# A fused attention and expert kernel: two weight transposes made one, two turns of k moved into the next stage, stores moved to the end of their own stage

## The chip, the cores and the metric

The kernel runs on one core of one Trainium2 chip. The metric is device time in microseconds (us) for one execution. Each core has five engines that run their own instruction queues: TensorE (PE, with weight loads, PEld, beside its matmuls), VectorE (DVE), ScalarE (ACT), GpSimd (POOL) and SyncE (SP). SP computes nothing here: it issues transfers. The transfers themselves are carried out by the core's 16 DMA engines. Queue q1 holds those that SP issues (transposes, stores), q0 those that POOL issues (loads from memory with a cast).

## What is computed

Sliding-window causal attention (window 64, 8 batches, 8 heads, 576 rows, head size 64), and then a feed-forward layer on its output, with `h * cos(h)` as its activation:

```python
scores = scale * np.matmul(q, k.transpose(0, 1, 3, 2))
mask = (rel >= 0) & (rel < window)            # rel = row - column
scores = np.where(mask, scores, -1e9)
attn = softmax(scores); attn_out = np.matmul(attn, v)
x = attn_out.transpose(0, 2, 1, 3).reshape(B * S, H * D)   # 4608 x 512
h = x @ w_in                                                # 512 x 2048
out = (h * np.cos(h)) @ w_out                               # 2048 x 512
```

## The kernel before

The 4608 rows of x are worked in nine tiles `mt` of 512 rows (`n_mt`), and a batch has nine blocks of 64 rows (`NU`). A tile is eight blocks, so tile `mt` holds the last blocks of batch `mt - 1` and the first ones of batch `mt`. Each tile from 1 on is a stage of `T = 32` units of a plan: 16 units for the first product with its sine and gate (`L487` to `L491`, `L716`, `L719`), and 16 for the second (`L730`; tiles 7 and 8, `FAST`, use a product of seven parts, `L577`). In the profile a stage lasts about 31 us. While stage `mt = b - 1` runs its products, the attention of batch `b` is worked beside it:

- `load_chunk` (`L177`) loads q and k of a batch by POOL, in five chunks of 128 rows. `load_v` (`L185`) does the same for v.
- `turn_q` and `turn_k` (`L259`, `L270`, by `turn`, `L236`) transpose the chunks with DMAs issued by SP, in three turns each (`TURNS`, `L41`): chunks 0 and 1, chunks 2 and 3, and the short chunk 4. The tile for a turned k, `kT`, has two buffers.
- `burst_scores` (`L307`) puts all scores of half a batch on TensorE in two bursts per stage, at 14.6 and 20.2 units. The first burst takes blocks 0 to 3, the second the others (for batch 3 block 4 comes first in it, elsewhere block 8 last). Block j reads k's blocks j - 1 and j, and a chunk has two blocks.
- The weights of a batch come in nine groups, "places" 0 to 8. For each, `g_max` (DVE), `g_exp` (ACT), `g_inv` (DVE), `g_norm` (POOL, `L383`) and `g_trans` (`L396`) follow at fixed lags, of which the last issues a transposing DMA from SP (`L406`) into a tile `wT`. Some groups go through TensorE instead (`direct`).
- `values` (`L415`) multiplies the transposed weights by v on TensorE at the end of a stage, and `put_x` casts the result into the next tile of x.
- `store` (`L497`) writes 256 rows of a finished tile from `out_sb`, which has three buffers, by SP.

What runs when is written out by hand. For tile 0 and batches 0 and 1 the order is the string `FIRST`, in which `Gm.n`, `Ge.n`, `Gi.n`, `Gn.n`, `Gc.n` are the steps of group n and `V.p` the values of head pair p. Batch 1's groups 13 (four units) and 14 (three units) are those of pair 2. From tile 1 on, `at(time, step)` puts a step in a plan, and `pump(time)` (`L594`), called between TensorE's matmuls, emits every step that is due, sorted by time. Each engine's queue is then worked strictly in that order. This holds for SP's queue too: a transfer that waits for its data holds up all that stand behind it.

At the end of a stage that starts at unit `base`, with batch `b` in work, SP's order before the change is: wT of places 0 to 3, q's three turns for batch `b + 1`, wT of places 4 and 5, k's three turns for batch `b + 1` (26.0, 26.2, 26.4), wT of places 6 and 7, then, over the border, wT of place 8 (31.23), and the two stores of the tile just finished (32.5 and 33.5). Batch 2 has times of its own.

The tiles `s` and `e` (scores and exponentials of a group, 2 KB a partition) have six buffers each.

Of the kernel before, what the change touches and what calls it, by code (L numbers as in the profile page):

```python
# [10 lines left out]
def _safe_warn(msg, *a, **kw):  # L11
# [4 lines left out]
BF16 = mybir.dt.bfloat16  # L16
# [7 lines left out]
NU = 9  # L24
NC, NP = 6, 96
GF = 4
# [6 lines left out]
T = 2 * Q  # L33
LAGS = (0.2, 1, 3, 3.2, 3.8)
# [32 lines left out]
)  # L67
# [3 lines left out]
def kernel(  # L71
# [23 lines left out]
    att = ctx.enter_context(tc.tile_pool(name="att", bufs=3))  # L95
# [17 lines left out]
    st = {}  # L113
# [127 lines left out]
    def blocks_of(x, b, p, lo, n):  # L241
        if b < 2:
            return by_pair(x)[:, p, 64 * lo:64 * lo + 64 * n].rearrange("d (a t) -> d a t", t=64)
        at_ = [PAIRS * 2 * (i // 2) + 2 * p + i % 2 for i in range(lo, lo + n)]
        return x.rearrange("d (a t) -> d a t", t=64)[:, at_[0]:at_[-1] + 1:at_[-1] - at_[0] or 1]
# [33 lines left out]
    groups = [[(0, p, j) for j in range(GF * g, GF * g + GF)] for p in range(PAIRS) for g in range(TU // GF)]  # L279
# [19 lines left out]
    last = n_listed + 4, n_listed + 5  # L299
    direct = set(range(n_first)) | {n_first + i for i in DIRECT} | set(last)  # L300

    def keys(b, p, j):
        lo, chunks = max(j - 1, 0), 2 if j else 1
        rhs = blocks_of(st["kA", b], b, p, lo, chunks)
        return rhs[:, ::-1, :] if j and j % 2 == 0 else rhs, chunks
# [76 lines left out]

    def g_norm(n, engine="p"):  # L383
        (e, _), rden = st.pop(("e", n)), st.pop(("r", n))
        w = att.tile([128, GF, 128], BF16, tag="w", name="w", bufs=8)
        u = len(groups[n])
        (nc.gpsimd if engine == "p" else nc.vector).tensor_tensor(out=w[:, 0:u], in0=e[:, 0:u], op=ALU.mult,  # L387
                                in1=rden[:, 0:u].unsqueeze(2).to_broadcast([128, u, 128]))
        st["w", n] = w

    def put_wT(n, wT):
        for i, (b, p, j, *h) in enumerate(groups[n]):
            for e in range(2):
                st["wT", (b, 2 * p + e, j, h[0]) if h else (b, p, j, e)] = wT[:, i, 64 * e:64 * e + 64]

    def g_trans(n):  # L396
        w, u = st.pop(("w", n)), len(groups[n])
        if n in direct:
            st["tw", n] = t_ps = ps_t.tile([128, GF, 128], BF16, tag="t", name="tw_ps")
            for i in range(GF if n == FILL[0] else 0):  # L400
                nc.tensor.transpose(t_ps[:, i], ident, ident)
            for i in range(u):
                nc.tensor.transpose(t_ps[:, i], w[:, i], ident)
            return
        wT = att.tile([128, GF, 128], BF16, tag="wT", name="wT", bufs=20)
        nc.sync.dma_start(out=wT[:, 0:u], in_=w[:, 0:u].rearrange("p u c -> p (u c)"), transpose=True)  # L406
        put_wT(n, wT)

    def g_put(n, engine=None):
        wT, u = att.tile([128, GF, 128], BF16, tag="wT", name="wT", bufs=20), len(groups[n])  # L410
# [82 lines left out]
    def skewed(mt, ks, n):  # L493
        for ff in range(SKEW):
            first(mt, ff, ks, n == 0, n == PAIRS - 1)
# [95 lines left out]
    def at(time, fn, *args):  # L591
        plan.append((time, len(plan), fn, args))
# [8 lines left out]
    for i, (b, jobs, banks) in enumerate(bursts):  # L601
        t = T * (b - 1)
        at(t + BURST[i % 2] + 0.9 * (i == 1), burst_scores, i)
        for n in range(jobs[0][0], jobs[-1][-1] + 1):
            place = (n - n_listed) % NU
            time = t + BURST[0] + PACE * place
            lags = LAGS[:2] + tuple(t + T - 0.79 - time + 0.01 * s for s in range(3)) if place == NU - 1 else LAGS
            if b == 2 and place > 3:
                lags = tuple(max(x, y - time) for x, y in zip(lags, {4: (53.2, 53.5, 0, 0, 0), 5: (0,) * 5, 6: (0, 0, 60.96, 60.97, 61.5), 7: (0, 0, 61.1, 61.2, 61.8), 8: (61, 61.3, 0, 0, 0)}[place]))
            for lag, fn in zip(lags, (g_max, g_exp, g_inv)):  # L610
                at(time + lag, fn, n)
            at(time + lags[3], g_norm, n, "d" if n == n_listed + 5 else "p")
            if n in last:
                at(T * b - 4.1 + (n == last[1]), g_trans, n)
                at(T * b - 4.05 + (n == last[1]), g_put, n)
            else:
                at(time + lags[4], g_trans, n)

    for b in range(2, B):
        t0 = T * (b - 1)  # L620
        for lo, hi in TURNS:
            at(t0 - (2.01 - 0.1 * lo if b == 2 else T - (24.3 if b == 4 else 23.4) - 0.01 * lo), turn_q, b, lo, hi)
        if b > 2:
            for c in range(NB):
                for i, name in enumerate(("q", "k")):
                    time = 17.9 + 2.8 * i if b == 3 and c == NB - 1 else 5.6 + 1.6 * c + 0.8 * i
                    if name == "k" and (b == 3 or c > 2):
                        time = ((24.31 if c > 1 else 13) if b == 3 else 24.2 if b == 4 else 22.4) + 0.01 * c
                    if b > 4 and c == 0:
                        time = (24.26 if b == 5 else 22.46) + 0.01 * i - T  # L630
                    at(t0 - T + time, load_chunk, name, b, c)
        for lo, hi in TURNS:
            at(t0 + 0.1 * lo - (2 if b == 2 else 6), turn_k, b, lo, hi)
        for c in range(5):
            at(t0 + (8 if b == B - 1 else 0.5) + c, load_v, b, c)
        for half_ in range(2):
            if b == 2:
                at(t0 + 24.1 + 0.01 * half_, spread_v, b, half_, "p", 0, 2)
                at(t0 + 24.2 + 0.1 * half_, spread_v, b, half_, "p", 2, 4)
            else:  # L640
                at(t0 + (24 if b == 3 else 22.2) + 0.1 * half_, spread_v, b, half_)
    for mt in range(2, n_mt):
        for p in range(PAIRS):
            time = T * mt - (8.01 if mt == n_mt - 1 else 1.01)
# [55 lines left out]
    for mt in range(1, n_mt):  # L700
        base = mt * T
        gT = []
        for ks in range(PAIRS):
            pump(max([base - 1] + [time for time, _, fn, args in plan if fn is put_x and args[:2] == (mt, ks)]))
            skewed(mt, ks, ks)
        for ff in range(n_ff):
            for ks in range(PAIRS):
                if ff >= SKEW:
                    first(mt, ff, ks, ks == 0, ks == PAIRS - 1)
            h_ps = st.pop(("h", ff))  # L710
            sin = moe.tile([128, MT], F32, tag="sin", name="sin", bufs=4)
            if ff % 2 == 0:
                gt = moe.tile([128, 2, MT], BF16, tag="gT", name="gT", bufs=n_ff // 2 + 2)
                gT.append(gt)
            e = ff % 2
            nc.scalar.activation(sin, h_ps, AF.Sin, bias=math.pi / 2.0)  # L716
            if ff == n_ff - 1 and mt < B - 1:
                exp_table()
            nc.vector.tensor_tensor(out=gt[:, e], in0=h_ps, in1=sin, op=ALU.mult)  # L719
            pump(base + ff)  # L720
        if mt in FAST:
            fast_second(mt, gT)
            continue
        for ms0 in range(0, MT // 128, 2):
            o_sb = moe.tile([128, 2, d_model], F32, tag="out", name="out_sb", bufs=OUTS)
            o_ps = [bank(which, "out_ps") for which in (("O1",) if mt == n_mt - 1 and ms0 else ("O1", "O0"))]
            for e in range(2):
                ms = ms0 + e
                for ff in range(n_ff):
                    nc.tensor.matmul(out=o_ps[e], lhsT=gT[ff // 2][:, ff % 2, ms * 128:ms * 128 + 128],  # L730
                                     rhs=w_out_sb[:, ff], start=ff == 0, stop=ff == n_ff - 1)
                    if ff % 4 == 3:
                        if ff == n_ff - 1:
                            copy("a" if e and (mt > 1 or ms0) else "d", o_sb[:, e], o_ps[e])
                            if mt == n_mt - 1:
                                store(o_sb, mt, ms0, e, 1)
                        pump(base + Q + 4 * ms0 + (e * n_ff + ff) // 4)
            if mt < n_mt - 1:
                at(base + T + 0.5 + ms0 / 2, store, o_sb, mt, ms0, 0, 2)


# [28 lines left out]
```

## Time and profile before

| | |
|---|---|
| Median of 3 runs | 299.97 us (299.54 to 304.29) |
| The profiled execution | 300.91 us, its span 299.1 us |
| TensorE busy | 290.5 us, 2767 matmuls |
| ACT, DVE, POOL busy | 232.1, 229.3, 205.1 us |
| SP's transposes: wT, qT, kT | 60, 18, 18 |
| SP's stores of 512 KB | 16 |
| Queue q0 (POOL's loads) | 18.06 MB |
| Queue q1 (SP's transfers) | 25.15 MB |

The profile is one execution with all times from the start of the span. A row of a view that looks at some instructions gives engine, operation and tile, how often, the least, median and greatest duration in ns, and the first and last start in us; "DMA to landing" below it gives the least, median and greatest time from the issue of those transfers to the moment when their data lies at the goal. In a timeline a row begins with start and length of a run of equal instructions, and in square brackets stands how long the engine sat idle before it and for whom. In rows of windows follow the busy times of PE, PEld, DVE, ACT and POOL, the granted clock, the share of the DMA engines (over 1 where two queues are served at once) and GB/s. Waits are given as the total, how often, and the longest.

### The profile page before, as it was taken

The page shows a single profiled execution, that of the slowest core. Times are in us where ns is not written, and L with a number is a line of the kernel's source. Part 1 is how long each engine was busy: PE and PEld are TensorE (multiplying, and loading weights), DVE is VectorE, ACT ScalarE, POOL GpSimd, SP SyncE. Part 2 cuts the span into 40 slices and gives each one's busy share as a digit, 9 for nine tenths or more (in the row PEclk, how much of TensorE's full clock was granted, in tenths as well). Part 3 has the DMA queues.
Part 4 walks back from the last instruction along what each step waited for, and adds up shares of the span by engine and source line. Part 5 has one row for each costly group of instructions (what it writes and reads, how often), then busy time and mean ns, then how long its engine had stood idle before and what let it go on. Part 6 is the DMA issues. An engine that isn't in the chain of part 4 may idle for free.

```text
span 299.1 us, 8146 instructions
## 1 busy us (share of the span) xinstructions
PE 290.5 (97%) x2767; PEld 158.6 (53%) x2767; DVE 229.3 (77%) x896; ACT 232.1 (78%) x781; POOL 205.1 (69%) x226
## 2 busy tenths in 40 slices
PE   8979999899999999999999999999999999999995
PEld 3658854544454444444454545444544454784485
DVE  4988887888887885788677866887588658986893
ACT  4998699687988799769987998699969997305700
POOL 9899558982799959994999499959997850000000
PEclk9999999999999999999999999999999999999999
DMA  7999999999999999999999999999999443003013
GB/s 145 176 203 192 193 191 146 131 144 159 221 172 114 160 198 176 136 172 235 160 156 153 233 137 171 143 232 155 158 143 161 72 88 143 0 2 141 3 35 105
DMA packets 168267, 43.79 MB, mean 146 GB/s; under 512 B 155617, under 2 KB 163873, under 8 KB 168225
## 3 DMA queue, kind: packets, MB, share of 16 engines
q0 software_dynamic: 100896, 18.06, 80.7%
q1 hardware_dynamic: 67184, 25.15, 47.6%
q8 instruction: 21, 0.34, 0.5%
q14 instruction: 22, 0.17, 0.2%
q10 hardware_dynamic: 144, 0.07, 0.1%
HBM read 36.70 MB, written 9.44 MB: 154 GB/s over the span
## 4 chain that ended last, share of the span: by engine, by line
PE 75%; DMA 11%; POOL 5%; DVE 3%; ACT 3%; issue 1%; POOLq 0%; DVEq 0%
PE h_ps L490 37%; PE out_ps L730 23%; PE out_ps L577 8%; DMA w_out<-in_moe_w_out_dram 7%; DMA wT<-w 3%; ACT e L370 2%; PE o_ps L422 2%; PE s_ps L321 2%; POOL w L387 2%; DMA q<-in_q_dram 2%; PE out_ps L473 1%; POOL v L188 1%; POOL w_in L204 1%; DVE s L358 1%; DVE v L126 1%
## 5 line engine op out<-in xcount | busy, mean ns | idle before, releaser
L490 PE MATMUL h_ps<-xT,w_in 128*128 128x512 bf16 x512 | 111.8, 379 | 0.2
L719 DVE TENSOR_TENSOR gT<-h_ps,sin 128x512 bf16<-128x512 f32 x128 | 84.8, 688 | 27.2 <-ACT sin L716 27.2
L716 ACT ACTIVATE sin<-h_ps 128x512 f32<-128x512 f32 x128 | 73.7, 599 | 33.2 <-PE h_ps L490 32.5
L370 ACT ACTIVATE e<-s,negm 128x128 f32<-128x128 f32 (+1 forms) x256 | 97.1, 382 | 2.2 <-DVE negm L358 1.2
L387 POOL TENSOR_TENSOR w<-e,rden 128x512 bf16<-128x512 f32 (+1 forms) x68 | 68.8, 1028 | 29.6 <-DVE rden L380 21.0
L730 PE MATMUL out_ps<-w_out,gT 128*128 128x512 bf16 x384 | 85.3, 379 | 0.0
L490 PEld LDWEIGHTS <-w_in 128*128 128x128 bf16 x512 | 50.1, 98 | 59.1
L730 PEld LDWEIGHTS <-gT 128*128 128x128 bf16 x384 | 36.5, 98 | 43.1
L358 DVE CUSTOM_DVE_ANT_0 s<-s_ps,mask 128x128 f32<-128x128 f32 (+1 forms) x256 | 56.0, 276 | 2.5 <-PE s_ps L343 2.0
L370 ACT ACTIVATION_READ_ACCUMULATOR e<-s,negm 128x1 f32 x256 | 48.1, 188 | 0.0
L188 POOL DMA_DIRECT2D v<-in_v_dram x40 | 34.1, 877 | 1.2 <-PE h_ps L490 0.8
L182 POOL DMA_DIRECT2D q<-in_q_dram x30 | 26.3, 892 | 3.9 <-issue 3.3
L380 DVE RECIPROCAL rden<-den 128x4 f32<-128x4 f32 (+1 forms) x73 | 12.1, 166 | 18.4 <-ACT e L370 18.2
L182 POOL DMA_DIRECT2D k<-in_k_dram x30 | 26.2, 885 | 0.0
L126 POOL COPY v<-v 64x1536 bf16<-64x1536 bf16 (+3 forms) x16 | 22.9, 1431 | 0.4
L358 DVE DVE_READ_ACCUMULATOR2_ANT negm<- 128x1 f32 x256 | 21.2, 83 | 0.0
L126 DVE CAST xT<-o_ps 128x512 bf16<-128x512 f32 x24 | 15.6, 679 | 6.4 <-PE o_ps L422 6.2
L473 PE MATMUL out_ps<-w_out,gT 128*128 128x512 bf16 x64 | 15.0, 379 | 0.3 <-DMA w_out<-in_moe_w_out_dram 0.2
L454 PE MATMUL h_ps<-xT,w_in 128*128 128x256 bf16 x128 | 14.8, 273 | 0.0
L126 ACT CAST xT<-o_ps 128x512 bf16<-128x512 f32 x12 | 7.0, 582 | 8.5 <-PE o_ps L422 8.0
L577 PEld LDWEIGHTS <-sums 128*128 128x128 bf16 x136 | 12.2, 98 | 1.9 <-DVE sums L522 0.4
L454 PEld LDWEIGHTS <-w_in 128*128 128x128 bf16 x128 | 12.2, 98 | 1.6 <-DMA w_in<-in_moe_w_in_dram 0.2
(90 smaller groups left out, 291.0 us busy)
## 6 DMA issues: line engine op xcount, KB each, us to landing
out_dram<-out_sb SPq DMA_DIRECT2D x16, 512.0 KB, 8.4
v<-in_v_dram POOLq DMA_DIRECT2D x32, 128.0 KB, 6.3
q<-in_q_dram POOLq DMA_DIRECT2D x24, 128.0 KB, 8.9
k<-in_k_dram POOLq DMA_DIRECT2D x24, 128.0 KB, 7.1
w_in<-in_moe_w_in_dram POOLq DMA_DIRECT2D x4, 512.0 KB, 9.3
w_out<-in_moe_w_out_dram POOLq DMA_DIRECT2D x4, 512.0 KB, 11.4
q<-in_q_dram POOLq DMA_DIRECT2D x7, 144.0 KB, 5.9
k<-in_k_dram POOLq DMA_DIRECT2D x7, 144.0 KB, 6.0
```

What stands on the lines that cost most here:

```text
L126: {"a": nc.scalar.copy, "p": nc.gpsimd.tensor_copy}.get(engine, nc.vector.tensor_copy)(out, in_)
L182: nc.gpsimd.dma_start(out=st[name, b][0:n, c].rearrange("p (h d) -> p h d", h=H), in_=src.rearrange("h p d -> p h d"))
L188: nc.gpsimd.dma_start(out=vt.rearrange("p (h d) -> p h d", h=H), in_=v[b, :, c * 128:c * 128 + n, :].rearrange("h p d -> p h d"))
L358: nc.vector.tensor_tensor_reduce(out=s[:, u, c], in0=s_ps[:, u, c], in1=mask[:, 2 - j % 2 if j else 0, c], scale=-scale if b else -1.0, sc ...
L370: nc.scalar.activation(e[:, u, c], s[:, u, c], AF.Exp, bias=negm[:, u:u + 1], scale=1.0 if n < n_first else -1.0, accum_out=den[:, u:u + 1])
L387: (nc.gpsimd if engine == "p" else nc.vector).tensor_tensor(out=w[:, 0:u], in0=e[:, 0:u], op=ALU.mult, in1=rden[:, 0:u].unsqueeze(2).to_br ...
L454: nc.tensor.matmul(out=h_ps[:, half * e:half * e + half], lhsT=w_in_sb[:, ks, ff * 128:ff * 128 + 128], rhs=st["xT", 0][:, ks, half * g:ha ...
L490: nc.tensor.matmul(out=st["h", ff], lhsT=w_in_sb[:, ks, ff * 128:ff * 128 + 128], rhs=st["xT", mt][:, ks], start=start, stop=stop)
L577: nc.tensor.matmul(out=to[n_] if split else to[:, e], lhsT=lhs[name][f // 2][:, f % 2, 128 * e:128 * e + 128], rhs=rhs[name][:, f, lo:hi], ...
L716: nc.scalar.activation(sin, h_ps, AF.Sin, bias=math.pi / 2.0)
L719: nc.vector.tensor_tensor(out=gt[:, e], in0=h_ps, in1=sin, op=ALU.mult)
L730: nc.tensor.matmul(out=o_ps[e], lhsT=gT[ff // 2][:, ff % 2, ms * 128:ms * 128 + 128], rhs=w_out_sb[:, ff], start=ff == 0, stop=ff == n_ff - 1)
```

## The change

Three things change.

Batch 1's groups 14 and 13 share one tile of weights, group 14 in units 0 to 2 and group 13 in units 3 to 6, and one transposing DMA of seven units, issued where group 13's was (`Gc.14` goes from `FIRST`). The shared tile takes one buffer of `s`, its transposed form one of `e`.

Of k's three turns only the first stays at the end of the stage before (6 units before the border). The second and third are issued 1.8 and 2.0 units after the border, in the stage whose second burst of scores reads them. Batch 2's stay as they were.

Of a tile's two stores the first is issued at 26.5 units of its own stage, behind k's first turn and ahead of wT of places 6 and 7; the second at 0.5 units of the next stage (1.5 before). The wT of place 8 moves from just before the border to 0.91 units after it, behind that store. The tiles worked by `fast_second` keep their store times.

So SP's order at a border becomes: k's first turn, first store, wT of places 6 and 7, second store, wT of place 8, k's second and third turn.

```diff
@@ FIRST
-    "o.1.3 Gn.16.d Gi.15 Gn.15.d Gw.8 Gc.14 Gc.13 Lk2.0 Gp.8.d Gw.16 Lk2.1 Ge.17 Lk2.2 Gp.16.d Gi.17 Lk2.3 o.2.3 "
+    "o.1.3 Gn.16.d Gi.15 Gn.15.d Gw.8 Gc.13 Lk2.0 Gp.8.d Gw.16 Lk2.1 Ge.17 Lk2.2 Gp.16.d Gi.17 Lk2.3 o.2.3 "
...
+    joined = {14: 0, 13: len(groups[14]), -1: len(groups[14]) + len(groups[13])}
...
     def g_norm(n, engine="p"):
         (e, _), rden = st.pop(("e", n)), st.pop(("r", n))
-        w = att.tile([128, GF, 128], BF16, tag="w", name="w", bufs=8)
         u = len(groups[n])
+        if n in joined:
+            if "joined" not in st:
+                st["joined"] = att.tile([128, 2 * GF, 128], BF16, tag="s", name="w", bufs=6)
+            w = st["joined"][:, joined[n]:joined[n] + u]
+        else:
+            w = att.tile([128, GF, 128], BF16, tag="w", name="w", bufs=8)
...
-        wT = att.tile([128, GF, 128], BF16, tag="wT", name="wT", bufs=20)
+        if n in joined:
+            w, u = st["joined"], joined[-1]
+            wT = att.tile([128, 2 * GF, 128], BF16, tag="e", name="wT", bufs=6)
+        else:
+            wT = att.tile([128, GF, 128], BF16, tag="wT", name="wT", bufs=20)
         nc.sync.dma_start(out=wT[:, 0:u], in_=w[:, 0:u].rearrange("p u c -> p (u c)"), transpose=True)
-        put_wT(n, wT)
+        for m in joined if n in joined else ():
+            if m > 0:
+                put_wT(m, wT[:, joined[m]:])
+        if n not in joined:
+            put_wT(n, wT)
...
-            lags = LAGS[:2] + tuple(t + T - 0.79 - time + 0.01 * s for s in range(3)) if place == NU - 1 else LAGS
+            lags = LAGS[:2] + tuple(t + T - 0.79 - time + 0.01 * s for s in (0, 1, 170)) if place == NU - 1 else LAGS
...
         for lo, hi in TURNS:
-            at(t0 + 0.1 * lo - (2 if b == 2 else 6), turn_k, b, lo, hi)
+            at(t0 + 0.1 * lo - (2 if b == 2 else -1.6 if lo else 6), turn_k, b, lo, hi)
...
             if mt < n_mt - 1:
-                at(base + T + 0.5 + ms0 / 2, store, o_sb, mt, ms0, 0, 2)
+                at(base + (T + 0.5 if ms0 else 26.5), store, o_sb, mt, ms0, 0, 2)
```

## The prediction

> **What bounds the kernel now.** I read the page's head first, then what TensorE waited for, then SP's queue and its landings at the stage ends.
>
> ```profile
> span 299.1 us, 8146 instructions
> PE 290.5 (97%) x2767; PEld 158.6 (53%) x2767; DVE 229.3 (77%) x896; ACT 232.1 (78%) x781; POOL 205.1 (69%) x226
> PEclk9999999999999999999999999999999999999999
> DMA  7999999999999999999999999999999443003013
> PE o_ps L422 <- DMA wT<-w: 1.2, 3, 0.8
> ```
>
> TensorE is busy 290.5 of 299.1 us, so 8.6 us are idle, and only the 1.2 us on wT have to do with anything that the change moves. Nothing here can make the kernel faster by 2% (6.0 us, about what a measurement can tell from no change). The DMA row counts more: the DMA engines are busy to the ninth tenth or above until about 230 us. TensorE does not feel it, because every transfer that it needs is issued long before. So the question for each moved transfer is whether it still lands before TensorE comes to it.
>
> The next rows are SP's issues at the end of tile 3 (the first and last start in each) with their landings, TensorE's second burst of scores for batch 5, whose k is turned here, the load of the DMA engines (the column before the last is their share, of 2 queues), and POOL's norms.
>
> ```profile
> L239 SPq DMA_TRANSPOSE kT<-k x3: 1273/1277/1451, 154.2 to 156.9; - x3
> DMA to landing us min/median/max: 3.7/5.6/6.1
> L406 SPq DMA_TRANSPOSE wT<-w x3: 1292/1332/1476, 158.5 to 161.3; - x3
> DMA to landing us min/median/max: 6.7/7.2/7.8
> L499 SPq DMA_DIRECT2D out_dram<-out_sb x2: 522/540/558, 162.9 to 163.5; - x2
> DMA to landing us min/median/max: 8.4/8.9/9.4
> 170.41 0.86 PE L321 MATMUL s_ps<-kT,qT 64*64 64x128 bf16 x40
> 162.00:166.00 4.00, 4.00 (x49) 1.84 (x48) 3.31 (x6) 3.06 (x5) 3.84 (x5) 1.00 1.97 157
> L387 POOL TENSOR_TENSOR w<-e,rden x5: 1029/1030/1035, 150.4 to 154.4; 128x512 bf16<-128x512 f32 x5
> ```
>
> SP issues one transfer about every 1.4 us, but they land every 2 us: the first k turn at 154.2 + 3.7 = 157.9, the third at 156.9 + 6.1 = 163.0, the third wT at 161.3 + 7.8 = 169.1, the second store at 163.5 + 9.4 = 172.9. That is 5.1 us for two turns, 6.1 for three wT, 3.8 for two stores, 15.0 in all, in the order of issue. Meanwhile POOL's loads keep the engines at a DMA share of 1.97, so this is a backlog, not a wait in the sequencer. Today its tail is two stores, which nobody waits for. The second burst, which reads turns two and three, starts at 170.4, with 7 us to spare.
>
> **The joined groups.** Removed: one transposing DMA of three units, and one issue on SP. The rows are TensorE's values for tile 1, SP's issues, the landings of the last two wT, and the norms.
>
> ```profile
> 56.09 0.66 PE L422 MATMUL o_ps<-wT,v 128*64 128x64 bf16 x30 [0.75 <-DMA wT<-w]
> 43.96 9.31 SPq L406 DMA_TRANSPOSE wT<-w  x6
> L406 SPq DMA_TRANSPOSE wT<-w x1: 1202/1202/1202, 50.7 to 50.7; - x1
> DMA to landing us min/median/max: 3.2/3.2/3.2
> L406 SPq DMA_TRANSPOSE wT<-w x1: 1245/1245/1245, 52.0 to 52.0; - x1
> DMA to landing us min/median/max: 4.0/4.0/4.0
> L387 POOL TENSOR_TENSOR w<-e,rden x4: 817/1031/1040, 45.7 to 51.4; 128x512 bf16<-128x512 f32 x3, 128x384 bf16<-128x384 f32 x1
> ```
>
> SP issues six transposes back to back from 44.0 on. The last, group 13, goes at 52.0 and lands at 56.0, where TensorE has waited 0.75 us. Its norm is the third of these four on POOL; a copy of about 1 us stands between it and the norm of 51.4, so it is done by about 50.4 and the wait is for SP's turn. Joined, the transfer goes in group 14's place at 50.7. No row has seven units. The three-unit one took 3.2 us and the four-unit one 4.0; if they ran wholly one after the other their size would add at most 56.0 - 53.9 = 2.1 us to 53.9, so it lands between 53.9 (50.7 + 3.2) and 56.0. I take the low half of this, since 1.3 us of the difference is the later issue: the whole 0.75 us goes, with 0 as the other end. What is late next is nothing in this stage: the values of pair 3 come through TensorE's own transposes. The two borrowed buffers cost nothing: the e and s tiles that they displace hold groups whose work is done before 51 us, and their next users belong to batch 2's first burst, which stands behind tile 1's first product in TensorE's order.
>
> **Tile 1's end (batch 3).** This stage end differs, because SP itself is held up.
>
> ```profile
> 87.96 10.15 SPq L239 DMA_TRANSPOSE kT<-k  x3
> L239 SPq DMA_TRANSPOSE kT<-k x2: 1237/1459/1681, 95.1 to 96.4; - x2
> DMA to landing us min/median/max: 6.3/6.5/6.8
> L499 SPq DMA_DIRECT2D out_dram<-out_sb x2: 494/526/558, 102.4 to 103.1; - x2
> DMA to landing us min/median/max: 9.1/9.6/10.2
> 102.73 0.59 PE L321 MATMUL s_ps<-kT,qT 64*64 64x64 bf16 x32
> 108.53 0.86 PE L321 MATMUL s_ps<-kT,qT 64*64 64x128 bf16 x40
> 119.22 0.98 PE L422 MATMUL o_ps<-wT,v 128*64 128x64 bf16 x50 [0.29 <-DMA wT<-w]
> ```
>
> The first turn goes at 88.0 and the second only at 95.1: it waits for k's loads, and three wT and two stores stand behind it until 98.1 (88.0 + 10.15). After the change those five go first, into the gap, and the turns go at about 95 to 97 as now, but behind five transfers of 2 us. If the first turn has landed by 95.1, as I take it, the same 15 us give about 110 for the third, 1.5 us after the second burst begins; that burst begins here with a group that needs the second turn only, and the group that needs the third is its last, so I take 0.5 us (ends 0 and 2.5). In return the backlog before the first burst's wT ends at 110 in place of 113.2 (103.1 + 10.2), and the wait at 119.2 and a shorter one just before it (1.2 - 0.75 = 0.45 us together) go. Sum of this stage: 0. The first burst also shows that a burst waits for its own turns and not for the whole kT tile: it ran at 102.7, and the third turn landed at 96.4 + 6.8 = 103.2.
>
> **The ends of tiles 2, 3, 4 and 5 (batches 4 to 7).** Each store and each second burst has its rows here, that of batch 5 stands above.
>
> ```profile
> L499 SPq DMA_DIRECT2D out_dram<-out_sb x2: 466/508/550, 132.8 to 133.5; - x2
> DMA to landing us min/median/max: 8.5/8.9/9.4
> 139.94 0.86 PE L321 MATMUL s_ps<-kT,qT 64*64 64x128 bf16 x40
> L499 SPq DMA_DIRECT2D out_dram<-out_sb x2: 532/615/698, 193.5 to 194.3; - x2
> DMA to landing us min/median/max: 8.7/9.2/9.7
> 200.93 0.86 PE L321 MATMUL s_ps<-kT,qT 64*64 64x128 bf16 x40
> L499 SPq DMA_DIRECT2D out_dram<-out_sb x2: 468/495/522, 222.0 to 222.6; - x2
> DMA to landing us min/median/max: 3.9/5.6/7.3
> 231.40 0.86 PE L321 MATMUL s_ps<-kT,qT 64*64 64x128 bf16 x40
> ```
>
> All of it is issued by SP; POOL's queue is passed by nothing. Behind the first k turn SP now issues: the first store (its copy was made some three units of the plan before), wT of places 6 and 7 (their norms end by 155.4 with the others), then from the next stage the second store, the wT of place 8, and turns two and three. No step waits in SP, so no one is held up behind a waiting instruction there; the third turn's issue moves behind five others, from 156.9 to about 162. But the transfers land in the order of issue, and the same seven now end with the two turns: 157.9 + 3.8 + 6.1 gives 167.8 before them, and 5.1 more is 172.9 for the third turn. That is where the second store lands now. TensorE comes to that burst at 170.4 and needs the third turn for its last group, and perhaps sooner, as its waits stand in order. So it waits about 172.9 - 170.5 = 2.4 us. The same step for batch 4: 133.5 + 9.4 = 142.9 less 140.0, 2.8 us; for batch 6: 194.3 + 9.7 = 204.0 less 201.0, 2.9 us. For batch 7 the tail lands at 222.6 + 7.3 = 229.9, before 231.4: nothing, with 1.5 us to spare.
>
> The ends for each wait: 0, if the turns behind the stores run without the loads beside them, and about 4, if the stores in front slow the loads and the loads then crowd the turns. I stay near the sum, less 0.4 us each for batches 5 and 6, because a wait in a second burst delays neither POOL's loads nor q's turns of that stage, so these come earlier against its end. So 2.8 + 2.0 + 2.5 = 7.3 us. Stores earlier and place 8's wT later gain and cost nothing of their own: out_sb has three buffers and no row shows a wait on one, and place 8's weights are first read at the end of the stage that they now start in, over 20 us later.
>
> **Sum.** -0.75 + 0 + 7.3 = +6.55 us. The profiled execution took 300.91 us for its span of 299.1, which is 0.94 above the median of the three runs, 299.97. So 307.5 us for an execution like the profiled one, and 306.5 against the median.
>
> **The rivals.** First, on the other side, the turns land in time. It takes each of the seven transfers to be served in 84% of the time shown, (170.5 - 157.9) / 15.0. Batch 7's end speaks for it, where the same seven are through before the burst. Against it speaks the DMA share of 1.97, which the loads make and which the change leaves. Then only the gains remain, -0.75 and -0.45 us: 298.8 us.
>
> Second, the waits are there but short, about 1 us each, as the loads of a stage that has become longer are out of the way: 299.97 - 0.75 + 3, about 302 us.
>
> Third, the waits feed on themselves, since TensorE's clock falls after an idle stretch. The clock row shows nines throughout, but the longest of the waits above is 0.8 us, so no row has one as long as the new ones. What follows the second burst until the values is 40 matmuls at 8.74 us in the chain:
>
> ```profile
> 171.28 8.74 PE out_ps L730 x40
> ```
>
> At half clock this would take up to 8.7 us more in each of three stages; a third of it in each is 8.7 us on top, 315 us. The Trainium skill, page TensorE: Matmul & The Clock Gate, section Part 1: The HAM clock gate (the "warmup" mystery), says that after one idle window of about 3.4 us the matmul clock falls to half and needs as long a busy one to come back; by its figure a wait of 2.8 us should mostly stay below that, and one that trips it would cost, as an estimate, some 1.7 us more. No run here shows it yet.
>
> **How the numbers follow.** The forecast (three waits of 1.5 to 3.5 us) gets 0.58, the first rival 0.24, the second 0.13, the clock 0.05. The likeliest has 304 to 309 us as its own range. The range reaches from 299.0, to take in most of the first rival, to 309.0; the clock and the tails stay out. Slower by over 2% means above 306.0: two thirds of the forecast's 0.58 and the clock, 0.44. Faster by over 2% (under 294.0) is more than TensorE has idle time for in reach, 0.01. The rest, 0.55, is within 2%.
>
> **What would show it.** In the changed profile: the wait at 56 us gone or under 0.2; the line of TensorE's burst (L321) waiting for a DMA on kT, three times, 2 to 3 us each, in the second burst of batches 4, 5 and 6, and none in batch 7's; a SP queue at each stage end with a store between the first k turn and the wT, and the last turn landing 10 us or more after its issue. Wrong it is if SP's transfers land in another order than they are issued, if the turns behind the stores take well under 5 us, or if TensorE's waits appear at a first burst.

## The result, and the profile after

The changed kernel takes 310.32 us in the median of 5 runs (307.99 to 311.92). The kernel before, run on the same chip, took 300.12 us (299.54 to 304.29). The ratio is 1.0331 with a 95% interval of 1.0285 to 1.0377: 3.3% slower, 10.2 us. The forecast was slower, 306.5 us; the time lies above its range, which ended at 309.0. (Ratios leave out disturbed executions, so one can differ a little from the quotient of two medians.)

The profiled execution of the changed kernel took 310.32 us, its span 308.5 us. The head of its page:

```profile
span 308.5 us, 8136 instructions
PE 293.9 (95%) x2767; PEld 160.6 (52%) x2767; DVE 230.4 (75%) x896; ACT 233.3 (76%) x781; POOL 205.2 (66%) x226
PEclk9979999999999999997999999999999999999999
```

The span is 9.4 us longer than before. TensorE does the same 2767 matmuls, but is busy 3.4 us longer for them and idle 6.0 us longer. The clock row has a new 7 in its nineteenth slice (138.8 to 146.5 us). The 7 in the third slice (15.4 to 23.1 us) lies ahead of everything that the change moves, and e10, the same kernel, does not have it.

What TensorE waited for (total, times, longest), and its timeline around the second bursts of batches 4, 5, 6 and 7:

```profile
PE s_ps L323 <- DMA kT<-k: 7.2, 4, 4.2
PE s_ps L323 <- DVE rden L382: 1.0, 1, 1.0
143.07 0.91 PE L323 MATMUL s_ps<-kT,qT 64*64 64x128 bf16 x32 [4.20 <-DMA kT<-k]
144.25 0.63 PE L323 MATMUL s_ps<-kT,qT 64*64 64x128 bf16 x8 [0.27 <-DMA kT<-k]
144.82 5.40 PE L745 MATMUL out_ps<-w_out,gT 128*128 128x512 bf16 x20
176.68 0.64 PE L323 MATMUL s_ps<-kT,qT 64*64 64x128 bf16 x32 [1.20 <-DMA kT<-k]
178.28 0.41 PE L323 MATMUL s_ps<-kT,qT 64*64 64x128 bf16 x8 [0.96 <-DVE rden L382]
209.97 1.13 PE L323 MATMUL s_ps<-kT,qT 64*64 64x128 bf16 x40 [1.56 <-DMA kT<-k]
240.70 0.86 PE L323 MATMUL s_ps<-kT,qT 64*64 64x128 bf16 x40
```

Three bursts wait, where they ran without a gap before, and the fourth does not. The waits are 4.47, 2.16 and 1.56 us. Each burst takes what it can: 32 matmuls when the second turn has landed, the last 8 when the third has. The row at 178.28 names VectorE, whose reciprocal (L382) ended at 178.15; k's third turn landed at 178.1 (168.7 + 9.4). In the kernel before, the 40 matmuls of a burst do not wait for VectorE, so this wait is read as one for the turn. The 20 matmuls at 144.82 take 270 ns each, where the chain before showed 8.74 / 40 = 218 ns.

SP's issues at the border between tiles 2 and 3, where k of batch 4 is turned, and the landings of the first turn (first two rows) and of the other two (last two):

```profile
123.16 1.25 SPq L239 DMA_TRANSPOSE kT<-k  x1
124.52 0.52 SPq L514 DMA_DIRECT2D out_dram<-out_sb  x1
125.14 3.19 SPq L417 DMA_TRANSPOSE wT<-w  x2
128.43 0.76 SPq L514 DMA_DIRECT2D out_dram<-out_sb  x1
129.28 2.09 SPq L417 DMA_TRANSPOSE wT<-w  x1
131.48 4.68 SPq L239 DMA_TRANSPOSE kT<-k  x2
L239 SPq DMA_TRANSPOSE kT<-k x1: 1255/1255/1255, 123.2 to 123.2; - x1
DMA to landing us min/median/max: 4.2/4.2/4.2
L239 SPq DMA_TRANSPOSE kT<-k x2: 1591/2294/2997, 131.5 to 134.6; - x2
DMA to landing us min/median/max: 9.6/10.6/11.5
```

The order is the one described: first turn, store, two wT, store, wT, two turns. The first turn lands at 123.2 + 4.2 = 127.4, the second at 131.5 + 11.5 = 143.0, the third at 134.6 + 9.6 = 144.2. The seven transfers behind the first turn therefore took 16.8 us. For batches 5 and 6 the same reading gives 18.0 and 17.1 us.

Where the time went, stage by stage. A stage runs from the first matmul of a tile's first product to that of the next tile; for tile 3 these are the rows

```profile
118.75 1.02 PE L505 MATMUL h_ps<-xT,w_in 128*128 128x512 bf16 x4
155.70 1.02 PE L505 MATMUL h_ps<-xT,w_in 128*128 128x512 bf16 x4
```

so 36.95 us. All stages, read in the same way:

| us | start of tile 1 | tile 1 | tile 2 | tile 3 | tile 4 | tile 5 | tile 6 |
|---|---|---|---|---|---|---|---|
| before | 57.90 | 30.92 | 31.41 | 30.47 | 30.51 | 30.48 | 30.51 |
| after | 57.27 | 30.92 | 30.56 | 36.95 | 32.92 | 32.37 | 30.51 |
| difference | -0.63 | 0 | -0.85 | +6.48 | +2.41 | +1.89 | 0 |

The differences add up to 9.3 of the 9.4 us. The three stages whose second burst works on batches 4, 5 and 6 hold all of the loss, and the first of them holds three fifths (6.48 of 10.78).

### The profile page after: what moved, and what is told of

Its sections match the earlier page's. It is cut to its first block, busy times and chain, and to the rows that moved or that the text cites. A ratio compares the mean times of both kernels' runs of the same rounds, so it can differ in the third digit from the quotient of the medians.

```text
span 308.5 us, 8136 instructions
## 1 busy us (share of the span) xinstructions
PE 293.9 (95%) x2767; PEld 160.6 (52%) x2767; DVE 230.4 (75%) x896; ACT 233.3 (76%) x781; POOL 205.2 (66%) x226
## 4 chain that ended last, share of the span: by engine, by line
PE 61%; DMA 19%; POOL 9%; ACT 5%; DVE 3%; issue 3%; SPq 0%; POOLq 0%
PE h_ps L505 29%; PE out_ps L745 15%; PE out_ps L592 8%; DMA kT<-k 7%; DMA w_out<-in_moe_w_out_dram 6%; ACT e L372 3%; PE out_ps L488 3%; POOL w L394 3%; DMA wT<-w 3%; DMA v<-in_v_dram 2%; PE o_ps L437 2%; PE s_ps L323 1%; POOL v L188 1%; DVE s L360 1%; POOL q L165 1%
## 5 line engine op out<-in xcount | busy, mean ns | idle before, releaser
L505 PEld LDWEIGHTS <-w_in 128*128 128x128 bf16 x512 | 50.0, 98 | 59.6 <-issue 0.5
L382 DVE RECIPROCAL rden<-den 128x4 f32<-128x4 f32 (+1 forms) x73 | 12.1, 166 | 19.9 <-ACT e L372 19.0
L323 PE MATMUL s_ps<-kT,qT 64*64 64x128 bf16 (+1 forms) x432 | 9.8, 222 | 8.3 <-DMA kT<-k 7.2
L323 PEld LDWEIGHTS <-qT 64*64 64x64 bf16 x432 | 7.6, 109 | 13.7 <-issue 12.4
```

Source lines behind the costliest of these rows:

```text
L505: nc.tensor.matmul(out=st["h", ff], lhsT=w_in_sb[:, ks, ff * 128:ff * 128 + 128], rhs=st["xT", mt][:, ks], start=start, stop=stop)
```

## The experiments

The theory: k's second and third turn stand behind the stores and the late wT in SP's order, and TensorE reaches the second burst before they land. Its rivals and open sizes: that the stores, put between the wT, are what delays them; that the clock adds a part of its own in tile 3; that the loads which POOL issues beside them, and not SP's order alone, make each transfer so long. The first four kernels are compared with 28 runs of the kernel before, with a median of 299.76 us.

**e1, the joined groups alone** (the changed kernel with turns, stores and place 8 put back):

```diff
-for s in (0, 1, 170))
+for s in range(3))
...
-(2 if b == 2 else -1.6 if lo else 6)
+(2 if b == 2 else 6)
...
-at(base + (T + 0.5 if ms0 else 26.5), store, o_sb, mt, ms0, 0, 2)
+at(base + T + 0.5 + ms0 / 2, store, o_sb, mt, ms0, 0, 2)
```

> The joined transpose alone; turns, stores and place 8 as before. Queue theory (what costs is where the late k turns stand in SP's in-order backlog): the wait of 0.75 us at 56 us goes, no wait on kT anywhere, each stage of tiles 1 to 6 as long as before (30.5 to 31.5 us), so 299.4 us, 0.6 below before. Rival (the shared s and e buffers cost something later): a wait of DVE or ACT on the shared buffers in batch 2's first burst, 300 us or more.

Measured: 300.27 us (12 runs), ratio 1.0022 [0.9996, 1.0049]. Joining alone gains nothing, and costs nothing that these runs can tell (the interval reaches from no change to 0.5% slower).

**e2, k's turns put back** (the changed kernel, stores and place 8 as changed):

```diff
-(2 if b == 2 else -1.6 if lo else 6)
+(2 if b == 2 else 6)
```

> The changed kernel with k's turns back at the end of the stage before; joined transpose, early stores and late place 8 stay. Queue theory: turns two and three stand right behind turn one again and land some 7 us before their burst, so no wait on kT, no drop of the clock, 298 to 300 us. Rival (stores between transposes slow SP's whole queue, whatever stands behind them): wT of places 6 to 8 land later than before, and some of the loss stays, 302 us or more.

Measured: 301.08 us (8 runs), ratio 1.0067 [1.0030, 1.0104]. No burst waits on k, and tiles 3 to 6 are back at 30.5 us. So the moved stores alone do not make the loss. What is left, 1 to 3 us by the interval and more than the 298 to 300 us expected, stands beside a wait of 0.8 us on wT at 119.3 us in its profile; its cause was not followed further.

**e3, the turns alone moved** (the kernel before, with this one line):

```diff
-(2 if b == 2 else 6)
+(2 if b == 2 else -1.6 if lo else 6)
```

> The kernel before with k's second and third turn moved alone: in the queue they now stand behind wT of places 6 to 8 and both stores, but no store stands between the wT. Queue theory: the same five transfers are ahead of them, so waits on kT in the second bursts of batches 4, 5 and 6 as in the changed kernel, 2 to 4 us each, 307 to 310 us. Rival (what slows is a store between transposes): the seven transfers take 15 us as in the kernel before instead of 17 to 18, waits shorter by 2 to 3 us each, 301 to 304 us and no drop of the clock.

Measured: 310.48 us (4 runs), ratio 1.0327 [1.0275, 1.0378]: the whole loss, with one line. SP's order and TensorE's second burst of batch 4 in its trace:

```profile
121.61 1.26 SPq L239 DMA_TRANSPOSE kT<-k  x1
122.96 4.13 SPq L406 DMA_TRANSPOSE wT<-w  x3
127.19 1.14 SPq L499 DMA_DIRECT2D out_dram<-out_sb  x2
128.43 5.61 SPq L239 DMA_TRANSPOSE kT<-k  x2
140.26 1.07 PE L321 MATMUL s_ps<-kT,qT 64*64 64x128 bf16 x32 [2.83 <-DMA kT<-k]
```

Here no store stands between the wT, and the loss is the same. It is enough that the five transfers are ahead of the two turns, in whichever order. Its profiled execution had waits for batches 4 and 6, and none for batch 5.

**e4, the turns ahead of both stores** (the changed kernel, with the stores behind k's turns):

```diff
-at(base + (T + 0.5 if ms0 else 26.5), store, o_sb, mt, ms0, 0, 2)
+at(base + T + 2.3 + ms0 / 10, store, o_sb, mt, ms0, 0, 2)
```

> The changed kernel with both stores of a tile issued behind k's third turn (2.3 and 2.5 units into the next stage); only wT of places 6 to 8 stand ahead of the turns. Queue theory: the turns land earlier by the service of two stores, 3.8 us or more, so of the waits of 4.5, 2.2 and 1.6 us at most the first leaves something, 299 to 301 us. Rival (the clock's drop or the turns' late issue itself is what costs, not what stands ahead): waits stay within 1 us of the changed kernel's, 306 us or more.

Measured: 299.54 us (10 runs), ratio 0.9997 [0.9975, 1.0020].

```profile
124.57 4.11 SPq L417 DMA_TRANSPOSE wT<-w  x3
128.78 3.23 SPq L239 DMA_TRANSPOSE kT<-k  x2
132.12 1.12 SPq L514 DMA_DIRECT2D out_dram<-out_sb  x2
138.81 0.86 PE L323 MATMUL s_ps<-kT,qT 64*64 64x128 bf16 x40
PE s_ps L323 <- DMA kT<-k: 1.0, 1, 1.0
```

With three transfers ahead of the turns in place of five, batch 4 does not wait, and one wait of 1.0 us on k is left in the whole execution (batch 5). So the turns can be issued after the border, as long as the stores go behind them. That is worth nothing either, but it shows that the place in the queue decides.

The next kernels look at tile 1's end, the clock and v's loads, against 23 runs of the kernel before (median 299.86 us).

**e5 and e8, the moves at tile 1's end only,** with the joined groups (e5) and without them (e8). Both restrict the three moves to batch 3's turns, tile 1's stores and batch 2's place 8; e5 starts from the changed kernel (its edit is shown), e8 from the one before:

```diff
-for s in (0, 1, 170))
+for s in (0, 1, 170 if b == 2 else 2))
...
-(2 if b == 2 else -1.6 if lo else 6)
+(2 if b == 2 else -1.6 if lo and b == 3 else 6)
...
-at(base + (T + 0.5 if ms0 else 26.5), store, o_sb, mt, ms0, 0, 2)
+at(base + (T + 0.5 + ms0 / 2 if mt != 1 else T + 0.5 if ms0 else 26.5), store, o_sb, mt, ms0, 0, 2)
```

> The changed kernel with the move of turns, stores and place 8 kept at the border behind tile 1 alone (batch 3), the joined transpose kept; all other borders as before. Queue theory: no wait on kT in batches 4 to 6, tile 2's stage shorter by 0.85 us as in the changed kernel's profile: 298.5 to 300 us. Rival (every stage with moved turns loses): batch 3's second burst waits too, 301 us or more.

> The kernel before with turns, stores and place 8 moved at the border behind tile 1 alone, and no joined transpose. If the joined transpose gains 0.75 us, this stays 0.75 us above the version that has it; if it gains nothing, both are within 0.3 us of each other. 298.9 to 299.7 us.

Measured: 300.28 us, ratio 1.0012 [0.9983, 1.0040], and 301.60 us, ratio 1.0017 [0.9981, 1.0053], 12 runs each. At this border the moves are neutral, as far as intervals of about 1 us to either side can tell, and no difference by the joined groups shows. In e8's profile TensorE runs its values at 54.8 us in one piece, without the joined groups:

```profile
54.79 1.28 PE L422 MATMUL o_ps<-wT,v 128*64 128x64 bf16 x64
```

So the 0.75 us in front of them, which the profile of before showed at 56 us, belonged to that execution and not to the kernel.

**e6, TensorE kept busy through the wait of batch 4** (the changed kernel, with 14 matmuls whose result is overwritten by the scores):

```diff
             st["s", g] = s_ps.rearrange("p (u c) -> p u c", c=128)
+            for _ in range(14 if n == 5 and g == jobs[0][0] else 0):
+                nc.tensor.matmul(out=s_ps, lhsT=w_out_sb[:, 0, 0:128], rhs=w_out_sb[:, 0], start=True, stop=True,
+                                 skip_group_check=True)
```

> The changed kernel with 14 matmuls of 512 columns, 3.0 us, put on TensorE just ahead of batch 4's second burst, into a scores bank that the burst then overwrites: they fill most of its wait of 4.2 us. Clock theory: TensorE has no idle stretch over about 1.5 us there, the clock stays at full rate in that stage, tile 3's stage gets some 1.8 us shorter (36.9 to about 35.1), 308 to 309.5 us. Rival (no time is lost to the clock; the wait alone costs): tile 3's stage stays within 0.5 us of 36.9, 310 us.

Measured: 307.26 us (4 runs), ratio 1.0280 [1.0217, 1.0342]. The window of the four microseconds behind the wait, in the changed kernel (first row) and in e6 (second):

```profile
143.00:147.00 4.00, 3.66 (x46) 1.93 (x46) 2.91 (x26) 1.65 (x8) 2.32 (x2) 0.57 1.95 155
143.00:147.00 4.00, 3.84 (x21) 1.87 (x20) 1.86 (x17) 3.06 (x16) 3.89 (x3) 1.00 1.66 162
```

The granted clock is 0.57 in the first and 1.00 in the second. Tile 3 shrinks from 36.95 to 34.64 us, and the total is below the 308 to 309.5 us expected. Not all of this is the clock's: in e6 the second turn also landed earlier in its stage, for the burst begins 23.18 us after the stage's start (141.50 - 118.32) and in the changed kernel 24.32 us (143.07 - 118.75). The clock's part is what differs behind the last eight scores. In e6 they and the start of the next stage are

```profile
142.65 0.41 PE L326 MATMUL s_ps<-kT,qT 64*64 64x128 bf16 x8 [0.51 <-DMA kT<-k]
152.96 13.97 PE L508 MATMUL h_ps<-xT,w_in 128*128 128x512 bf16 x62
```

so 10.31 us, against 11.45 us in the changed kernel (144.25 to 155.70): 1.1 us are the clock's. A second comparison on another chip, the changed kernel again (**e10**) beside the filled one again (**e11**):

> The changed kernel once more, beside the next run on the same chip. 308 to 312 us, the longest wait in batch 4's second burst, over 3.5 us, with the clock at half for 3.4 us behind it.

> The 14 matmuls in front of batch 4's second burst once more, beside the changed kernel itself. Clock theory: 1.5 to 2.5 us below it, the clock at full rate in tile 3's stage. Rival (no loss to the clock): within 0.5 us of it.

Measured: 311.29 us (ratio 1.0337 [1.0266, 1.0408]) and 308.99 us (1.0285 [1.0227, 1.0344]), 4 runs each, before 301.21. Tile 3 took 36.31 us in e10 and 34.78 in e11. The medians differ by 2.3 us, but the two intervals overlap, and in e10's profile the clock fell a second time, in batch 6's stage (the last section has its rows). So the medians do not give the clock's price; the stages do. From the last eight scores to the stage's end e11 has the same 10.31 us as e6 (143.80 to 154.11). In e10, whose clock in the window from 143 to 147 us was 0.65 (e11: 1.00), the burst and what follows it took 12.44 us (142.21 to 154.65), against 10.76 in the kernel before (139.94 to 150.70). A spell of half clock thus cost 1.1 to 1.7 us here, out of the 6.48 us of tile 3.

**e7, v's loads 8 to 12 units later** (the changed kernel, batches 4 to 6):

```diff
-at(t0 + (8 if b == B - 1 else 0.5) + c, load_v, b, c)
+at(t0 + (8 + c if b == B - 1 else 12.1 + 0.1 * c if b > 3 else 0.5 + c), load_v, b, c)
```

> The changed kernel with the five loads of v for batches 4 to 6 issued at 12.1 to 12.5 units of their stage in place of 0.5 to 4.5, so behind the loads of q and k in POOL's queue. Contention theory (the seven transfers take 17 to 18 us because POOL's loads share the DMA engines with them): fewer loads run beside them, the turns land 3 us or more sooner, waits on kT in the three bursts together under 4 us against 8.2, 302 to 306 us. Rival (SP's queue serves one transfer every 2 us or more whatever runs beside it): waits stay at 7 to 9 us, 309 to 311 us.

Measured: 309.63 us (4 runs), ratio 1.0328 [1.0276, 1.0381], with 6.1 us of waits on k, between the two expectations. It does not separate them: with v's gone from the front of POOL's queue, its loads of q and k went there at once, so the load beside SP's transfers was only exchanged (between 127 and 144 us the packets of POOL's queue q0 took 111.8% of the span of the 16 DMA engines, against 105.3% in the changed kernel).

**e9, v's loads of batches 4 to 6 left out** (the values of these batches are then worked with an older v):

```diff
-at(t0 + (8 if b == B - 1 else 0.5) + c, load_v, b, c)
+if b not in (4, 5, 6):
+    at(t0 + (8 if b == B - 1 else 0.5) + c, load_v, b, c)
```

> The changed kernel without the loads of v for batches 4, 5 and 6 (their outputs are worked with an older v): nothing else is removed, SP's queue and POOL's other work stay. This leaves POOL six loads of q and k beside the seven transfers in place of eleven. Contention theory: the seven land in 13 us or less in place of 17 to 18, waits on kT in the three bursts together 3 us or less, no drop of the clock, 302 us or less. Rival (one transfer of SP's queue per 2 us or more whatever else runs): the third turn still lands 15 us or more after the first, waits of 6 us or more, 307 us or more.

Measured: 307.65 us (2 runs), ratio 1.0235 [1.0155, 1.0315]. The seven transfers took 16.2, 14.4 and 15.0 us, not the 13 or less of the first expectation and mostly under the 15 or more of its rival; batch 4 still waited 4.0 us. The loads of q and k again moved up, and between 127 and 143 us q0's packets still took 103.1% of the engines' span, though they carried 0.71 MB in place of 1.05. So this run does not separate the two either.

**e12, all loads behind the turns** (the changed kernel; v's loads of batches 4 to 6 and the loads of q and k for batches 5 to 7 are issued after the second burst):

```diff
-at(t0 + (8 if b == B - 1 else 0.5) + c, load_v, b, c)
+at(t0 + (8 + c if b == B - 1 else 21.3 + 0.05 * c if b > 3 else 0.5 + c), load_v, b, c)
...
-5.6 + 1.6 * c + 0.8 * i
+5.6 + 1.6 * c + 0.8 * i if b < 5 else 21.6 + 0.05 * c + 0.02 * i
```

> The changed kernel with POOL's loads of v for batches 4 to 6, and of q and k for batches 5 to 7, issued 21.3 to 21.9 units into their stage, behind the second burst, in place of 0.5 to 12. Nothing runs beside the seven transfers then; the end of each stage gets longer, since these loads come late for it, so the total time says nothing. Contention theory (the loads are what makes one transfer take 2 us and more): in batches 4 to 6 the third turn lands 10 us or less behind the first, and no second burst waits on kT. Rival (SP's queue is that slow by itself): 14 us or more, and the waits stay.

First come k's turns at the border between tiles 2 and 3: first turn with its landing, then the other two with theirs. Then the second bursts of batches 4, 5 and 6, and the two longest waits of the execution:

```profile
L239 SPq DMA_TRANSPOSE kT<-k x1: 1249/1249/1249, 125.9 to 125.9; - x1
DMA to landing us min/median/max: 4.7/4.7/4.7
L239 SPq DMA_TRANSPOSE kT<-k x2: 1248/1302/1355, 133.0 to 134.3; - x2
DMA to landing us min/median/max: 3.4/3.8/4.3
140.96 0.86 PE L323 MATMUL s_ps<-kT,qT 64*64 64x128 bf16 x40
180.26 0.86 PE L323 MATMUL s_ps<-kT,qT 64*64 64x128 bf16 x40
218.89 0.86 PE L323 MATMUL s_ps<-kT,qT 64*64 64x128 bf16 x40
PE o_ps L437 <- POOL v L126: 13.1, 3, 6.1
PE s_ps L323 <- DMA kT<-k: 4.3, 1, 4.3
```

The first turn lands at 125.9 + 4.7 = 130.6, the third at 134.3 + 4.3 = 138.6. The same seven transfers, in the same order, now take 8.0 us (7.9 and 9.2 at the next two borders), and none of the three bursts waits. That is about the pace at which SP issues them (8.4 us from the first turn's issue to the third's). The queues between the two landings, in the changed kernel (first two rows, 127 to 144 us) and here (last row, 130 to 139 us, where no row of q0 exists); the percentage is the time of the packets as a share of the 16 engines' span:

```profile
q0 software_dynamic: 8289, 1.05, 105.3%
q1 hardware_dynamic: 3467, 1.66, 69.6%
q1 hardware_dynamic: 3594, 1.78, 77.4%
```

The single run took 325.69 us: the loads themselves are now late, and TensorE waits 13.1 us for v at three stage ends and 4.3 us for k of batch 7. It is no better kernel, but it separates the two causes. SP's order decides what stands ahead of the turns; the loads beside them double what the seven cost together.

No version tried is faster than the kernel before; e4 (0.9997) and e5 (1.0012) equal it.

## Why the prediction was right and wrong

**The mechanism was right.** The prediction said that TensorE would wait for k in the second bursts of batches 4, 5 and 6, and not in batch 7's, with the last turn landing 10 us or more after its issue, behind stores and wT. This is in the profile (11.5 us from issue to landing for batch 4's second turn, 9.6 for the third, a little under what was said), and e3, e4 and e2 show that the turns' place behind those transfers is the cause. The first rival (the turns land in time, 298.8 us) and the second (waits of about 1 us, 302 us) are out. "0, if the turns behind the stores run without the loads beside them", given as the lower end of each wait, is what e12 showed.

**The step that failed is the size of batch 4's term: 2.8 us predicted, 6.48 measured.** The prediction took "the same seven" to need 15.0 us in any order, so that the third turn would land where the second store had landed; it set this against the old start of the burst, and it put the clock at nothing in its sum. Three things came out otherwise. The seven took 16.8 us. TensorE was at the burst 1.1 us earlier than before (143.07 - 4.20 = 138.87, before 139.94), because gaps earlier in the profile of before were missing here. Together these two made the waits 4.47 us. The third is the third rival, to which the prediction gave 0.05: the clock fell behind this wait, for 3.4 us, and cost another 1.1 us (11.45 against 10.31 us behind the last scores). It did so in one of the three stages, and in two of them in e10, not in all as the rival had it. Of the 0.9 us that remain, 0.3 stand ahead of the stage's first burst; the rest was not followed.

The Trainium skill, page TensorE: Matmul & The Clock Gate, section Part 1: The HAM clock gate (the "warmup" mystery), has the clock fall after an idle window of about 3.4 us and come back after as long a busy one. The spells of the changed kernel have that length, and the estimate of 1.7 us made from it is what e10's second spell cost (12.00 us from batch 6's last scores at 210.13 to the stage's end at 222.13, against 10.31). Batch 4's cost less, since part of it ran while TensorE waited for the third turn anyway. What failed is the reading that a wait of 2.8 us would mostly not trip the clock: batch 4's wait was 4.2 us, and in e3 a wait of 2.83 us tripped it too.

Two smaller points of the working: from the rows shown, 142.9 - 140.0 is 2.9 and 204.0 - 201.0 is 3.0, a tenth more each than the prediction has, which changes nothing. And the DMA share of 1.97 is not a share out of 2, as it reads there: a window of e3 below has 3.01, and q0 alone has 105.3%. It did not show how near to a limit the engines were.

**Batches 5 and 6: 2.0 and 2.5 us predicted, 2.41 and 1.89 measured.** These are about right, but by two errors that offset each other. The seven transfers took 18.0 and 17.1 us and not 15, while the first turn landed earlier in its stage: for batch 5 4.4 us after tile 4's start (155.70) against 7.2 before, probably because the long stage in front of it had let the loads of k finish; no run tested that.

**Batch 7: 0 predicted, 0 measured.** Its burst at 240.70 runs without a gap.

**Tile 1's end: 0 predicted, and e5 and e8 agree** (1.0012 and 1.0017). But the prediction had a wait there for the third turn, landing at about 110 us, and a gain that made up for it. In the changed kernel the turn landed at 107.1 (98.6 + 8.5), ahead of the burst at 107.90; the seven took 12.4 us at this border. In the trace tile 2 is 0.85 us shorter. But e1, which moves nothing there, also has 30.47 us, and e2 31.80: the short waits on wT at 119 us come and go between executions.

**The joined groups: -0.75 us predicted, none found.** The same mistake: a wait that one execution showed was taken for one that the kernel has. The profiled execution had been 0.94 us above the median, and its waits on wT came to 1.2 us. Against the median there was nothing to win, as far as e1 and e8 tell, which makes the sum by stages fit: 6.48 + 2.41 + 1.89 = 10.8 us where 7.3 were predicted, and the medians differ by 10.2.

## What to carry to other kernels

Where a transfer is moved behind others in an engine's order, count the transfers that then stand ahead of it and price each by what it costs beside the loads that run at that time; leave room over the sum, because that price did not stay the same when the order changed (15.0 us for seven transfers before, 12.4 to 18.0 after). A wait on TensorE can cost more than itself, since the clock may fall behind it: here it did behind waits from 1.7 us up, but not behind each of them. A wait under 1 us in a single profile is no gain to be had until a second execution shows it too.

## What the runs showed of the hardware that was not expected

**How little idle time brings the clock down.** In the changed kernel an idle stretch of 4.20 us was followed by half the clock for 3.4 us. In e3 waits of 2.83 and 2.31 us (each followed by one more, of 1.44 and 1.82) were enough, and the spells were twice as long, 6.8 us. The windows of e3 around the first two of these waits (columns as before, the granted clock third from the end):

```profile
140.00:144.00 4.00, 2.30 (x42) 1.53 (x42) 2.77 (x25) 1.65 (x8) 1.97 (x2) 0.50 3.01 113
144.00:148.00 4.00, 4.00 (x14) 1.56 (x13) 0.14 (x2) 1.27 (x6) 3.94 (x5) 0.71 1.37 199
```

In e10, the changed kernel again, two waits of 1.69 and 0.28 us in batch 6's burst were enough: the matmuls behind them take 430 ns each (first three rows). In e11 waits of 2.00 and 0.25 us in the same burst were not: there the matmuls behind them take 220 ns (last two rows).

```profile
209.22 0.64 PE L323 MATMUL s_ps<-kT,qT 64*64 64x128 bf16 x32 [1.69 <-DMA kT<-k]
210.13 0.41 PE L323 MATMUL s_ps<-kT,qT 64*64 64x128 bf16 x8 [0.28 <-DMA kT<-k]
210.48 3.01 PE L745 MATMUL out_ps<-w_out,gT 128*128 128x512 bf16 x7
207.56 0.64 PE L326 MATMUL s_ps<-kT,qT 64*64 64x128 bf16 x32 [2.00 <-DMA kT<-k]
208.79 8.81 PE L748 MATMUL out_ps<-w_out,gT 128*128 128x512 bf16 x40
```

The waits of 1.20 + 0.96 and of 1.56 us in the changed kernel left the clock at full speed as well. So the length of a wait alone does not tell whether the clock falls; no run here shows what else decides it. The same page and section of the Trainium skill ask for an idle window of about 3.4 us. The lengths of the spells (3.4 and 6.8) agree with such a window, but in e3 and e10 the clock fell with less than a whole window of idleness.

**What the loads do to SP's transfers.** 8.0 us for seven transfers alone, 16.8 to 18.0 beside POOL's loads, with the same bytes. The Trainium skill, page DMA: Bandwidth & Descriptors, section Queues, rings and completion order, says that a DMA engine takes turns between the queues that have work for it, packet by packet. The doubling fits that, though no run here looked at single packets.

**An issue on SP that grows.** The second turn of batch 4, issued behind the backlog, took 3.0 us on SP in the changed kernel (2997 ns above), batch 4's turns in e12 1.25 to 1.36. No run tells what holds them.
